# Spare rows of the direct key tiles carry 48 further key columns, with new planner thresholds

## The chip, the core and the metric

The kernel runs on one core of a Trainium2 chip. The metric is the device time of one execution in microseconds (us), the median of several runs. The engines work side by side, each through its own fixed list of instructions, and wait for each other by semaphores: TensorE (PE in the profile: matmuls; PEld: its weight loads), VectorE (DVE), ScalarE (ACT), GpSimd (POOL), and SyncE (SP), which issues the DMAs.

## What is computed

One transformer block in bf16 on 2048 tokens of width 640, with 32 heads of 20 columns and an MLP of width 1536. Six vectors from a conditioning vector scale, shift and gate its two halves:

```python
mod = (_silu(c) @ w_mod).reshape(c.shape[0], 6, 1, -1)
sa, ca, ga, sb, cb, gb = (mod[:, 0], ..., mod[:, 5])
h = _layernorm(x) * (1 + ca) + sa
qkv = h @ wqkv                       # 3 x 32 heads x 20
p = softmax(q @ k^T * 20 ** -0.5)    # per head, 2048 x 2048
x = x + ga * ((p @ v) @ wo)
h = _layernorm(x) * (1 + cb) + sb
x = x + gb * (((h @ w_gate) * (h @ w_up)) @ w_down)
```

## The kernel before

**Layout.** Heads are handled in 8 sets of four. In the tile KT the four heads of a set j lie in four strips of 32 partitions, 20 of which hold the head's key columns; QT is laid out likewise, and its 12 spare rows in each strip are zero, so whatever stands in the 12 spare rows of KT is multiplied by zero. Queries come in 7 blocks (CHUNKS: 512 tokens, then six of 256), keys in 4 token blocks tc of 512. An item is one set of one query block.

**The stream of exponentials.** For each item TensorE makes scores (L1824) into two pairs of PSUM banks. ScalarE takes the exponential of two banks in one instruction (L2801) and writes bf16 into a ring PP of 16 slots. A fixed part of the scores goes to VectorE and GpSimd instead (L1851, L1887, L1895, L1892, L1907), which form the exponential from integer operations into the tiles DB and DSS. TensorE multiplies both by the values Vf (L2504) and so frees the slots. When an item is complete, VectorE transposes and normalises it (L1978, L1984, L1989, L2021) into Ocp.

**Dense work.** Everything else on TensorE is cut into rounds: several steps that accumulate in one PSUM bank, then an evacuation by VectorE (or by ScalarE, when it has nothing else). There are rounds for the transposed activations hT (L1390), for keys and queries, for values (wV), for the gates (wmb), and for each query block a suffix: output projection (wo), layer norm, gate and up projection (stg or stx), down projection (wd), store. Rounds of column-tiled matmuls (L1233, L1429, L1493) run four strips of 32 columns side by side. The last block's suffix uses whole matmuls (L1229), and its layer-normed and transposed input is the tile h2Tc.

**How keys get into KT.** Set 0 is direct: `kq_round` (L1429) multiplies hT by four strips of 32 weight columns, each beginning at a head's first column, and the evacuation (L1442, L1443) writes the result straight into KT. The 12 extra columns of a strip are the first columns of the next head, and nobody uses them. The other seven sets are packed: `packed_round` (L1493) makes 128 columns at a time, five steps a round, from column k_base on; VectorE copies them to KPA (L1502), SP writes them to a scratch in HBM (k_rows, L1539), and one read for each set and token block brings them back in the layout of KT (L1557). With k_base = 80 there are 560 columns left: four blocks of 128 and one of 48 for each token block. A read waits for all writes of its token block issued so far.

**The order of the work.** The order of every engine's list is decided when the program is built, by a planner (class Sched) that plays the kernel through event by event with assumed durations. Whenever TensorE is free, it chooses: the next score visit, a dense piece (`pick_x`) or value products (`pv_issue`). Thresholds steer this choice. XFIRST puts dense pieces first while at least so many slot pairs of PP are free; XCONT does it for a round already begun; HOLD lets TensorE wait for a score bank soon to come free; PVMIN, PVMAX, PVCAP and PVTOL size a batch of value products. STAGE gives thresholds by item, and SEGT overrides them in segments of SEG = 8 exponentials, about 100 in all. Dense rounds have a queue key, need(x) = 13 + 10x with x in items, and a gate: the number of exponentials that must have been planned first. The packed key round of block b and token block tc has x = j0 + tc/4 - K_LEAD with K_LEAD = 0.652, where j0 is the first set that needs the block; value rounds of the second part have x from 2.02 up; the gate rounds (wmb) 2.32 and 2.37. Ten query rounds (LATEQ) and all suffix rounds have higher keys, and run in what is left.

Of the kernel before, what the change touches and what calls it, by code (L numbers as in the profile page):

```python
# [7 lines left out]
ALU = mybir.AluOpType  # L8
# [483 lines left out]
def emit_program(nc, sched, nsem_dma=56):  # L492
# [286 lines left out]
    1: {"PVTOL": 152.9, "XFIRST": 5},  # L779
    2: {"EAGER": 5},  # L780
    3: {"LKTOL": 409.9, "PVMAX": 4},
    5: {"HOLD": 18.3, "X_HALF": 186.9},
    6: {"PVCAP": 10, "PVTOL": 128.9, "XCONT": 2, "XDPRIO": 1.229},
    7: {"D_LATE": 18, "D_RES": 15, "HOLD": 49.8, "PVCAP": 18},
    9: {"HOLD": 75.5, "XBACK": 2},
    10: {"EAGER": 14, "HOLD": 75.5, "TPRIO": 0.516, "XBACK": 0},
    11: {"EAGER": 11, "PVTOL": 20.3, "XCONT": 3, "XG": -8},
    12: {"EAGER": 6, "PVTOL": 25.5, "XDPRIO": 1.926},
    13: {"HOLD": 90.7, "XG": 9},
    14: {"PV_OPEN": 1, "XBACK": 2, "XCONT": 6, "XG": -2},  # L790
    16: {"EAGER": 11, "PVTOL": 31.8, "XCONT": 4},
    17: {"D_RES": 22, "PVTOL": 373.5, "STEAL_GAP": 131.6},
    18: {"D_RES": 22, "LKTOL": 422.8, "PVMAX": 8, "PVMIN": 7, "PVTOL": 373.5, "STEAL_GAP": 131.6},
    20: {"PVTOL": 309.1, "XCONT": 0, "XG": 9},
    21: {"HOLD": 53.2, "PVMIN": 3, "PVTOL": 86.9},
    22: {"D_RES": 49, "PVCAP": 6},
    24: {"HOLD": 52.6},
    25: {"D_LATE": 13, "PV_KEEP": 3},
    26: {"EAGER": 12, "STEAL_GAP": 219.1, "XCONT": 5},
    27: {"XBACK": 2, "XG": -5},  # L800
    28: {"XCONT": 4},
    29: {"D_RES": 18, "EAGER": 15, "HOLD": 1.1, "XFIRST": 2},
    31: {"PVMAX": 6, "XDPRIO": 0.985},
    33: {"XCONT": 2, "XG": 3},
    34: {"HOLD": 14.4, "PVTOL": 187.4},
    36: {"D_LATE": 18, "EAGER": 8, "TPRIO": 0.426},
    37: {"D_LATE": 18, "EAGER": 8, "TPRIO": 0.426, "XCONT": 3},
    38: {"D_LATE": 18, "EAGER": 8, "HOLD": 14.3, "LKTOL": 40.3, "TPRIO": 0.723, "XCONT": 3, "XG": 4},
    39: {"D_LATE": 18, "EAGER": 8, "LKTOL": 40.3, "PV_OPEN": 3, "TPRIO": 0.723, "XCONT": 3, "XG": 4},
    40: {"EAGER": 6, "PVMIN": 6},  # L810
    41: {"EAGER": 3, "XFIRST": 3},
    42: {"EAGER": 4, "PV_OPEN": 1},
    43: {"XG": 14, "X_LATE": 69.8},
    44: {"EAGER": 14, "XFIRST": 5},
    45: {"EAGER": 14, "XFIRST": 5},
    46: {"D_LATE": 22, "D_RES": 20, "HOLD": 148.8},
    47: {"D_LATE": 22, "HOLD": 148.8, "PVMAX": 3, "XG": -2},
    48: {"EAGER": 2},
    49: {"EAGER": 5, "PVCAP": 15, "PV_KEEP": 4, "X_LATE": -212.0},
    50: {"EAGER": 11, "LKTOL": 38.6, "PVCAP": 15, "PV_KEEP": 4, "XDPRIO": 0.893, "X_LATE": -212.0},  # L820
    51: {"PVMIN": 5, "XBACK": 3, "XDPRIO": 0.768},
    52: {"HOLD": 97.6, "PV_OPEN": 3},
    53: {"XBACK": 2},
    54: {"HOLD": 148.1},
    55: {"PVMAX": 9, "PVMIN": 7, "PVTOL": 138.0, "TPRIO": 0.846},
    56: {"HOLD": 2.5, "PVMAX": 9, "PVMIN": 7, "PVTOL": 138.0, "PV_OPEN": 3, "TPRIO": 0.846, "X_HALF": 88.4, "X_LATE": -103.8},
    57: {"HOLD": 2.5, "PVMAX": 9, "PVMIN": 7, "PVTOL": 138.0, "PV_OPEN": 3, "TPRIO": 0.846, "X_HALF": 88.4, "X_LATE": -103.8},
    58: {"HOLD": 59.0},
    59: {"PVMAX": 4, "PV_KEEP": 1},
    60: {"PVCAP": 9, "XCONT": 2},  # L830
    61: {"LKTOL": 659.0, "PV_KEEP": 2},
    62: {"HOLD": 161.6, "XDPRIO": 1.236, "X_LATE": 20.3},
    64: {"PVCAP": 11, "PVMIN": 7, "XG": 10},
    65: {"EAGER": 10, "PVMIN": 3, "TPRIO": 0.795},
    66: {"HOLD": 0, "X_HALF": 144.4},
    67: {"EAGER": 14, "PVMAX": 13, "PV_KEEP": 2},
    68: {"EAGER": 5, "PVMAX": 13, "PV_KEEP": 2, "XG": -6, "X_LATE": 52.7},
    69: {"X_LATE": 187.0},
    70: {"HOLD": 9.6, "X_HALF": 37.7},
    72: {"HOLD": 202.6, "PV_OPEN": 3, "XDPRIO": 1.458},  # L840
    74: {"PVMIN": 5, "PV_KEEP": 4, "XG": 6},
    75: {"EAGER": 6, "HOLD": 0, "PVMIN": 2},
    76: {"LKTOL": 45.1, "PVMIN": 5, "PVTOL": 121.2},
    77: {"LKTOL": 45.1, "PVMIN": 5, "PVTOL": 121.2},
    81: {"X_LATE": 207.1},
    82: {"D_LATE": 37, "EAGER": 13, "XDPRIO": 0.618, "XFIRST": 2, "X_LATE": 207.1},
    83: {"XDPRIO": 1.036, "XFIRST": 4},
    84: {"STEAL_GAP": 206.3, "XCONT": 5},
    85: {"D_LATE": 5, "LKTOL": 647.8, "PV_KEEP": 4, "STEAL_GAP": 206.3, "XCONT": 5, "XG": 11},
    86: {"PVTOL": 117.5, "XBACK": 1, "XCONT": 2, "XFIRST": 4},  # L850
    87: {"PVMIN": 3, "PVTOL": 378.0, "XBACK": 0, "XCONT": 4},
    88: {"HOLD": 193.8},
    89: {"EAGER": 4, "HOLD": 193.8, "PVCAP": 17, "XG": -4},
    91: {"PVMIN": 3, "PV_KEEP": 2, "X_HALF": 0.7},
    93: {"PVCAP": 7, "PVMAX": 9, "X_LATE": -4.5},
    94: {"HOLD": 60.0, "PVCAP": 15, "PVMAX": 9, "X_LATE": -4.5},
    95: {"HOLD": 197.8, "PVCAP": 15, "PVMAX": 5, "PV_KEEP": 1, "X_LATE": -4.5},
    96: {"HOLD": 197.8, "PVCAP": 15, "PVMAX": 5, "PV_KEEP": 1, "XCONT": 5, "X_LATE": -4.5},
    97: {"PVMAX": 10},
    98: {"X_LATE": -11.0},  # L860
    99: {"PVMAX": 3, "XCONT": 3, "X_HALF": 4.5},
}
XG = 0
WO_GATE = 60
# [16 lines left out]
def build_kernel(nc, A_x, A_wqkv, A_wo, B_x, B_w_gate, B_w_up, B_w_down, c, w_mod, out):  # L881
# [197 lines left out]
    def dve(dur, f, deps=(), prio=3.0, **k):  # L1079
        return sc.add(Task("dve", dur, f, deps, prio=prio, **k))  # L1080
# [325 lines left out]
    kt_ready = {}  # L1406
    kt_half = {}
# [15 lines left out]

    def kq_round(kind, j, tc, prio, gate=0):
        wx = wk_sb if kind == "K" else wq_sb
        w0 = 80 * j
        mms = []
        for k in range(KD):
            f = [lambda e, b, k=k, s=s: e.matmul(  # L1429
                ps[32 * s:32 * s + 32, b, :], wx[:, k, w0 + DH * s:w0 + DH * s + 32], hT[tc][:, k, :],  # L1430
                tile_position=(0, 32 * s), start=(k == 0), stop=(k == KD - 1), skip_group_check=True) for s in range(4)]
            mms.append((C512, f))
# [29 lines left out]
        r = Round(mms, hd + w_deps(kind, j) + xd, after, prio, gate=gate, name=f"{kind}{j}.{tc}", pdeps=pd, split=split)  # L1462
# [16 lines left out]
    k_writes = {}  # L1479

    def k_base(tc):
        return 80 * KDJ if tc in K_DIRECT else 0
# [4 lines left out]
    def packed_round(kind, b, tc, prio, gate=0, late_q=False):  # L1487
# [59 lines left out]
        if kind == "K":  # L1547
            for j in range(NSET):
                top = min(80 * j + 91, D - 1)
                if 80 * j >= k_base(tc) and r0 <= top < r0 + w:  # L1550
                    dps = [x for l in done for x in l] + ([r_sb.last, r_cb.last] if j >= 4 else [])
                    kt_ready[(j, tc)] = [dma("sp", 32 * 1024, lambda e, j=j, s=s: e.dma_start(
                        KT[32 * s:32 * s + 32, j, tc * 512:(tc + 1) * 512],
                        KS[656 * tc + 80 * j + DH * s:656 * tc + 80 * j + DH * s + 32, :]),
                        dps, prio=1.1 + .01 * (j + tc / 4), dur=480.0) for s in range(4)]
                    for t in kt_ready[(j, tc)]:
                        t.whole = (kt_ready[(j, tc)], lambda e, j=j, tc=tc: e.dma_start(  # L1557
                            KT[:, j, tc * 512:(tc + 1) * 512],
                            bass.AP(KS.tensor, (656 * tc + 80 * j) * 512, [[DH * 512, 4], [512, 32], [1, 512]])))
# [476 lines left out]
    def suffix(ci):  # L2036
# [36 lines left out]
        for tl in range(ntl):  # L2073
# [30 lines left out]
            bn = []  # L2104
            for hf in range(2):
                bn.append(dve(ps_cost(320), lambda e, tl=tl, hf=hf: e.bn_stats(  # L2106
                    st2[:, tl, 6 * hf:6 * hf + 6], xck[:, tl, 320 * hf:320 * hf + 320]), [ev[hf]], prio=LN2T if tail else LN2P))
            ag = dve(115, lambda e, t=t, tl=tl: e.bn_aggr(mv2[:, t, :], st2[:, tl, :]), bn, prio=LN2T if tail else LN2P)
            f1 = lambda e, t=t: e.tensor_scalar(sd2[:, t:t + 1], mv2[:, t, 1:2], EPS, None, op0=ALU.add)
# [566 lines left out]
    def d_attach(ts, t, pos, rows, limit, relax):  # L2676
        n = 0
        got = []
        while n < limit:
# [34 lines left out]
            got.append((pick, b, st_, tu))  # L2714
# [4 lines left out]
        for pick, b, st_, tu in got:  # L2719
# [353 lines left out]
```

## Time and profile before

| what | value |
|---|---|
| median of 3 runs | 795.71 us (795.64 to 795.74) |
| the profiled execution | 795.55 us |
| its span | 793.8 us |
| dense key matmuls L1493, hT by wk | 360 |
| direct key matmuls L1429, hT by wk | 80 |
| granted TensorE clock | 1.0 in every slice |

The span runs from the first to the last instruction. The profile lists busy times of each engine, the chain of work that ended last, groups of instructions by line and shape, waits, and a timeline. All of these are from one execution, whose own time is the 795.55 us above. A matmul's duration is longer than the time by which it keeps the next one back, since matmuls are pipelined; what a matmul adds is read from the distance of successive ones.

### The profile page before, as it was taken

Reading aid. Unit: us, or ns where it says so; the run is one execution under the profiler, and the core shown is the slowest. Engines: PE = TensorE matmul, PEld = TensorE weight load, DVE = VectorE, ACT = ScalarE, POOL = GpSimd, SP = SyncE. Lnnn points to the kernel's source line nnn. Section 1 sums busy time; section 2 is a strip of 40 time slices with the busy share of each in tenths; the row PEclk is TensorE's granted clock in tenths of the full one; section 3 lists DMA queues with packets and bytes.
Section 4 is the critical chain, followed back from the end, with each engine's and each line's share of the span. In section 5 each row is a group of like instructions: output and inputs, shape, how many; then the busy total and the mean of one; then the engine's idle time right before and its main releaser. Section 6 shows DMA issues by size and latency. Waiting matters only on the chain.

```text
span 793.8 us, 36358 instructions
## 1 busy us (share of the span) xinstructions
PE 783.9 (99%) x16556; PEld 378.9 (48%) x16556; DVE 711.2 (90%) x1317; ACT 752.4 (95%) x837; POOL 358.1 (45%) x372
## 2 busy tenths in 40 slices
PE   8999999999999999999999999999999999999998
PEld 4433433333244444445455555545554455545567
DVE  7889888988999999989999989988999999898974
ACT  6999899999999999999999999999999999999941
POOL 3334646142466555444453536336355445353510
PEclk9999999999999999999999999999999999999999
DMA  9633222102351622110033305131430146214600
GB/s 301 218 111 98 63 61 61 60 25 71 107 130 43 198 46 52 44 36 20 11 94 69 70 19 117 40 68 36 102 86 21 33 105 135 62 38 91 137 20 19
DMA packets 146090, 61.88 MB, mean 78 GB/s; under 512 B 113215, under 2 KB 145935, under 8 KB 145935
## 3 DMA queue, kind: packets, MB, share of 16 engines
q1 hardware_dynamic: 145007, 58.40, 28.5%
q8 instruction: 130, 2.13, 1.1%
q10 hardware_dynamic: 928, 1.15, 0.4%
q14 instruction: 25, 0.20, 0.1%
HBM read 50.53 MB, written 8.99 MB: 75 GB/s over the span
## 4 chain that ended last, share of the span: by engine, by line
ACT 63%; PE 33%; DVE 3%; DMA 0%; issue 0%; SPq 0%
ACT PP L2801 63%; PE ps_all L1824 10%; PE ps_all L1233 8%; PE ps_all L2504 7%; PE ps_all L1493 3%; PE ps_all L1229 3%; DVE DB L1851 1%; DMA x<-in_A_x_dram 0%; PE ps_all L1429 0%; ACT xn L1300 0%; PE ps_all L1390 0%; PE ps_all L2148 0%; DVE DSS L1887 0%; PE ps_all L2966 0%; DVE st L2106 0%
## 5 line engine op out<-in xcount | busy, mean ns | idle before, releaser
L2801 ACT ACTIVATE PP<-ps_all 128x1024 bf16<-128x1024 f32 x798 | 734.6, 1169 | 4.8 <-PE ps_all L2504 2.6
L1907 POOL TENSOR_TENSOR DSS<-DB,DSS 128x512 bf16<-128x512 bf16 x252 | 287.0, 1159 | 309.3 <-DVE DSS L1895 227.1
L1851 DVE TENSOR_SCALAR DB<-ps_all 128x512 int16<-128x512 f32 x452 | 301.9, 683 | 40.3 <-PE ps_all L1824 38.4
L1824 PE MATMUL ps_all<-QT,KT 32*128 32x256 bf16 (+2 forms) x3648 | 315.3, 286 | 3.0 <-ACT PP L2801 1.0
L1824 PEld LDWEIGHTS ps_all<-QT,KT 32*128 32x128 bf16 x3648 | 92.2, 92 | 203.7 <-ACT PP L2801 182.5
L2504 PE MATMUL ps_all<-PP,Vf 128*32 128x256 bf16 (+4 forms) x2844 | 157.6, 290 | 0.3 <-DVE Vf L1593 0.2
L1233 PE MATMUL ps_all<-h2T,stg 128*32 128x256 bf16 (+2 forms) x2784 | 119.6, 279 | 0.2 <-DVE DB L1851 0.2
L2504 PE MATMUL ps_all<-DSS,Vf 128*32 128x256 bf16 (+1 forms) x1608 | 93.3, 288 | 0.1
L2504 PEld LDWEIGHTS ps_all<-PP,Vf 128*32 128x32 bf16 (+1 forms) x2844 | 58.6, 95 | 65.3 <-issue 56.7
L1887 DVE TENSOR_SCALAR DSS<-DB 128x2048 int16<-128x2048 int16 x113 | 79.2, 701 | 0.7
L1895 DVE TENSOR_SCALAR DSS<-DB 128x2048 int16<-128x2048 int16 x113 | 78.3, 693 | 1.2 <-PE ps_all L2504 1.2
L1233 PEld LDWEIGHTS ps_all<-h2T,stg 128*32 128x32 bf16 x2784 | 59.1, 96 | 36.3 <-issue 30.6
L1233 PE MATMUL ps_all<-wd,hprod 128*32 128x320 bf16 (+1 forms) x1364 | 62.3, 280 | 0.2
L1892 DVE TENSOR_TENSOR DSS<-DB,DSS 128x2048 bf16<-128x2048 bf16 x50 | 61.8, 1238 | 0.1
L2504 PEld LDWEIGHTS ps_all<-DSS,Vf 128*32 128x32 bf16 (+1 forms) x1608 | 40.5, 96 | 16.7 <-issue 9.0
L1989 POOL TENSOR_TENSOR OTn<-OT,invT 128x160 bf16<-128x160 f32 (+1 forms) x44 | 26.5, 622 | 44.3 <-DVE invT L1984 44.3
L1233 PEld LDWEIGHTS ps_all<-wd,hprod 128*32 128x32 bf16 x1364 | 31.0, 96 | 15.1 <-issue 11.4
L1233 PE MATMUL ps_all<-wV,hT 128*32 128x160 bf16 x1280 | 36.1, 234 | 0.0
L1493 PE MATMUL ps_all<-hT,wk 128*32 128x512 bf16 (+1 forms) x360 | 32.4, 382 | 0.0
L1493 PE MATMUL ps_all<-hT,wq 128*32 128x512 bf16 x375 | 31.3, 383 | 0.0
L1233 PE MATMUL ps_all<-wo,Ocp 128*32 128x320 bf16 (+1 forms) x656 | 30.2, 282 | 0.3 <-DVE DB L1851 0.2
L1233 PEld LDWEIGHTS ps_all<-wV,hT 128*32 128x32 bf16 x1280 | 23.4, 96 | 13.0 <-issue 8.3
(128 smaller groups left out, 513.8 us busy)
## 6 DMA issues: line engine op xcount, KB each, us to landing
stg<-in_B_w_gate_dram SPq DMA_DIRECT2D x74, 160.0 KB, 2.5
stg<-in_B_w_up_dram SPq DMA_DIRECT2D x74, 160.0 KB, 2.8
KT<-k_rows SPq DMA_DIRECT2D x28, 128.0 KB
QT<-q_rows SPq DMA_DIRECT2D x48, 64.0 KB, 2.1
wm<-in_w_mod_dram SPq DMA_DIRECT2D x3, 800.0 KB, 6.2
x<-in_A_x_dram SPq DMA_DIRECT2D x7, 320.0 KB
k_rows<-KPA SPq DMA_DIRECT2D x16, 128.0 KB, 2.7
wd<-in_B_w_down_dram SPq DMA_DIRECT2D x1, 1920.0 KB
```

The source lines that it names most:

```text
L1229: return lambda e, b: e.matmul(ps[:, b, c0:c0 + n], lhs(), rhs(), start=st, stop=sp)
L1233: return lambda e, b: e.matmul(ps[32 * x:32 * x + 32, b, c0 + o:c0 + o + w], lhs()[:, 32 * x:32 * x + 32], rhs() if w == n else rhs()[:, o ...
L1493: f = [lambda e, b_, k=k, x=x: e.matmul(ps[x:x + min(32, w - x), b_, :], wx[:, k, r0 + x:r0 + min(x + 32, w)], hT[tc][:, k, :], tile_posit ...
L1824: ems.append(lambda e, i=i, kt=kt: e.matmul(dstf()[:, i * u.n:(i + 1) * u.n], KT[32 * u.s:32 * u.s + 32, u.j, kt * 128:(kt + 1) * 128], QT ...
L1851: return e.tensor_scalar(DBl[st_["slot"]][:, x * 512:(x + 1) * 512], bank(cell["b"]), EBIAS, 0.0, op0=ALU.add, op1=ALU.max)
L1887: return e.tensor_scalar(DSl[st_["ss"][0]][:, :], DBl[st_["slot"]][:, :], 0x7F, 0x3F00, op0=ALU.bitwise_and, op1=ALU.bitwise_or)
L1892: return e.tensor_tensor(d, DBl[st_["slot"]][:, :].bitcast(BF16), d, ALU.mult)
L1895: return e.tensor_scalar(DSl[st_["ss"][1]][:, :], DBl[st_["slot"]][:, :], 0x7F80, 2, op0=ALU.bitwise_and, op1=ALU.bitwise_or)
L1907: return e.tensor_tensor(d, DBl[st_["slot"]][:, x * w:x * w + w].bitcast(BF16), d, ALU.mult)
L1989: return lambda e: e.tensor_tensor(OTn[:, g0:g0 + gn, DH * (j + x):DH * (j + x) + DH, :].rearrange("p b c r -> p b r c"), OT[:, nq_ * x:nq ...
L2504: ems.append(lambda e, i=i, kt=kt, stt=stt, stp=stp: e.matmul(ps[32 * s:32 * s + mc, binfo["bank"], c0:c0 + u.n], Vf[:, (kt * H + 4 * u.j ...
L2801: return e.activation(o, ps[:, b0:b0 + nu, :], AFT.Exp, scale=ESCALE)
```

## The change

The direct round of set 0 gets a weight tile of its own, wkp, in which the 12 spare columns of each strip hold columns 80 to 127 (12 for each of the four strips). Two GpSimd copies build it from wk once the first half of wk has landed. The evacuation is the same; the spare rows of KT now hold those 48 key columns, and four DMAs for each token block write them to their place in the scratch. The packed blocks start at column 128, and there are four of 128 for each token block. The first set that needs a block becomes 1, 3, 4, 6 (it was 1, 2, 4, 5, 7).

```diff
+WKP_PRIO = 0.5
+P1_TWO = 0
+KPACK = (0, 1, 2, 3)
+LN2_POOL = ()
...
+    wkp_c = []
+    wkp = alloc("wkp", [128, KD, 128], BF16) if KPACK else None
+
+    def pack_wk():
+        wkp4 = wkp[:, :, :].rearrange("p k (s c) -> p k s c", c=32)
+        for o, w, c0 in ((0, DH, 0), (DH, 32 - DH, 4 * DH)):
+            wkp_c.append(pool(KD * 4 * w * .9 + 150, lambda e, o=o, w=w, c0=c0: e.tensor_copy(
+                wkp4[:, :, :, o:o + w], wk_sb[:, :, c0:c0 + 4 * w].rearrange("p k (s c) -> p k s c", c=w)),
+                [d_wk[0]], prio=WKP_PRIO))
+
     def kq_round(kind, j, tc, prio, gate=0):
         wx = wk_sb if kind == "K" else wq_sb
         w0 = 80 * j
+        pk = kind == "K" and j == 0 and tc in KPACK
+        wst = DH
+        if pk:
+            wx, w0, wst = wkp, 0, 32
+            if not wkp_c:
+                pack_wk()
...
-                ps[32 * s:32 * s + 32, b, :], wx[:, k, w0 + DH * s:w0 + DH * s + 32], hT[tc][:, k, :],
+                ps[32 * s:32 * s + 32, b, :], wx[:, k, w0 + wst * s:w0 + wst * s + 32], hT[tc][:, k, :],
...
-        r = Round(mms, hd + w_deps(kind, j) + xd, after, prio, gate=gate, name=f"{kind}{j}.{tc}", pdeps=pd, split=split)
+        r = Round(mms, hd + (wkp_c if pk else w_deps(kind, j)) + xd, after, prio, gate=gate, name=f"{kind}{j}.{tc}", pdeps=pd, split=split)
+        if pk:
+            k_writes.setdefault(("K", tc), []).append([dma("sp", 12 * 1024, lambda e, s=s: e.dma_start(
+                KS[656 * tc + 80 + 12 * s:656 * tc + 92 + 12 * s, :],
+                KT[32 * s + DH:32 * s + 32, 0, tc * 512:(tc + 1) * 512]), list(r.evac), prio=1.0, dur=480.0) for s in range(4)])
...
     def k_base(tc):
-        return 80 * KDJ if tc in K_DIRECT else 0
+        return 128 if tc in KPACK else 80 * KDJ if tc in K_DIRECT else 0
...
-                if 80 * j >= k_base(tc) and r0 <= top < r0 + w:
+                if j >= (KDJ if tc in K_DIRECT else 0) and r0 <= top < r0 + w:
```

The table SEGT is replaced as a whole: 83 entries become 100, from a search that carries sixteen plans along. Entries with XFIRST above zero go from 8 to 17, with XCONT from 17 to 29, with PVMIN from 15 to 23; HOLD from 25 to 24, and EAGER stays at 25. Two lines of each as examples:

```diff
-    9: {"HOLD": 75.5, "XBACK": 2},
-    10: {"EAGER": 14, "HOLD": 75.5, "TPRIO": 0.516, "XBACK": 0},
+    9: {"EAGER": 15, "LKTOL": 462.9, "PVTOL": 356.7, "XFIRST": 3},
+    10: {"PVMIN": 5, "XBACK": 1, "XCONT": 3, "X_HALF": 134.5},
```

The diff also adds two branches that its own constants switch off: with LN2_POOL = () the second layer norm stays on VectorE, and with P1_TWO = 0 two score evacuations aren't joined into one.

More of the change, by code (lines that the diff above doesn't have):

```diff
@@ L2103, in suffix @@
             t = t0 + tl
[L2104 to L2109, printed above, removed]
@@ L2718, in d_attach @@
             n += 1
-        for pick, b, st_, tu in got:
+        if P1_TWO and len(got) == 2 and got[0][2] is got[1][2]:
+            got.sort(key=lambda g_: g_[0].quad[1])
+            (ua, ba, st_, ta, ra), (ub, bb, _, tb, rb) = got
+            if ba > bb:
+                ba, bb = bb, ba
+                ta.deps, tb.deps = unit_score_deps(ua) + rb, unit_score_deps(ub) + ra
+            (pa, ca), (pb, cb) = ua.task, ub.task
+            ca["b"], cb["b"] = ba, bb
+            ca["two"] = ((ba, ua.quad[1]), (bb, ub.quad[1]))
+            ca["pool"], ca["ks"] = G, (ba, bb)
+            pa.dur = ps_cost(1024)
+            pa.deps = [ta, tb] + st_["brel"]
+            for x in pb.users:
+                x.deps = [d for d in x.deps if d is not pb]
+                x.nleft -= 1
+            pb.users = []
+            st_["p1"][ub.quad[1]] = pa
+            sc.left -= 2
+            sc.add(pa)
+            return [ta, tb]
+        for pick, b, st_, tu, _ in got:
             tp, cell = pick.task
```

208 lines of the change are left out of this document (122 added, 86 removed).

## The prediction

> **What bounds the kernel now.** I read the page first: the span, the busy times, then the chain that ended last.
>
> ```profile
> span 793.8 us, 36358 instructions
> PE 783.9 (99%) x16556; PEld 378.9 (48%) x16556; DVE 711.2 (90%) x1317; ACT 752.4 (95%) x837; POOL 358.1 (45%) x372
> ACT 63%; PE 33%; DVE 3%; DMA 0%; issue 0%; SPq 0%
> L2801 ACT ACTIVATE PP<-ps_all 128x1024 bf16<-128x1024 f32 x798 | 734.6, 1169 | 4.8 <-PE ps_all L2504 2.6
> ```
>
> Two engines are full and the chain alternates between them: ScalarE with the exponentials (734.6 / 798 = 0.92 us each in the stream) and TensorE. So the question for each stretch is which of the two is late. The windows view, restricted to the exponentials (columns: window, its length, busy us and count), tells it:
>
> ```profile
> 20.00:40.00 20.00, 13.74 (x16) 1.00 0.70 221
> 80.00:95.00 15.00, 12.52 (x14) 1.00 0.24 66
> 95.00:217.00 122.00, 121.95 (x135) 1.00 0.21 61
> 217.00:307.00 90.00, 89.69 (x98) 1.00 0.38 102
> 307.00:762.00 455.00, 453.38 (x494) 1.00 0.28 64
> ```
>
> From 95 to 762 us exponentials run with 0.05 + 0.31 + 1.62 = 1.98 us of holes in 667. Nothing that TensorE saves there can be seen before the last exponential. Time can come only out of the start, the one hole at 80 to 95 us (2.48 us), and the tail behind the last exponential. The timeline of the hole and of the tail (start, length, instructions):
>
> ```profile
> 75.09 0.61 PE L1493 MATMUL ps_all<-hT,wk 128*32 128x512 bf16 x8
> 87.57 0.85 PE L1233 MATMUL ps_all<-wmb,SCb 128*32 128x320 bf16 x20
> 88.67 1.94 ACT L2801 ACTIVATE PP<-ps_all 128x1024 bf16<-128x1024 f32 x2 [1.87 <-PE ps_all L2504]
> 89.07 0.94 PE L1233 MATMUL ps_all<-wV,hT 128*32 128x160 bf16 x38
> 90.41 0.33 PEld L2504 LDWEIGHTS ps_all<-PP,Vf 128*32 128x32 bf16 x6 [0.38 <-DVE Vf L1593]
> ...
> 754.32 7.69 ACT L2801 ACTIVATE PP<-ps_all 128x1024 bf16<-128x1024 f32 x8
> 766.66 1.35 DVE L2138 TENSOR_SCALAR h2Tc<-ps_all,mcol 128x128 bf16<-128x128 bf16 x5 [0.21 <-PE ps_all L2126]
> 769.10 1.68 PE L1233 MATMUL ps_all<-wd,hprodt 128*32 128x320 bf16 x44
> 770.71 2.35 PE L1229 MATMUL ps_all<-h2Tc,stx 128*128 128x128 bf16 x39
> 773.34 17.79 PE ps_all L1229 x261
> ```
>
> The hole at 86.8 to 88.7: an exponential waits 1.87 us for the value product (L2504) to give back PP slots, and the product waits for V columns whose rounds (wV) are only then being run, behind dense key rounds (to 75.7) and the gate rounds (wmb). TensorE was late with dense work.
>
> The tail: the last exponential ends at 754.32 + 7.69 = 762.01. The input of the last block's MLP, h2Tc, is complete at 766.66 + 1.35 = 768.01, but its first matmul starts at 770.71, right behind the down-projection of the block before (wd, hprodt). From 770.71 TensorE is full to 773.34 + 17.79 = 791.13 (last row: the chain, by time). So leftover dense work delays the end by 770.71 - 768.01 = **2.70 us**. Is that leftover a backlog that reaches far back? The output stores of successive blocks (SP queue, by time) say yes:
>
> ```profile
> 542.01 9.13 SPq L2370 DMA_DIRECT2D out_dram<-xck  x2
> 616.06 14.20 SPq L2370 DMA_DIRECT2D out_dram<-xckb  x2
> 686.18 19.50 SPq L2370 DMA_DIRECT2D out_dram<-xck  x2
> 765.90 5.83 SPq L2370 DMA_DIRECT2D out_dram<-xckt  x2
> ```
>
> They end at 551.1, 630.3, 705.7 and 771.7: steps of 79, 75 and 66 us, while a block of about 98 exponentials takes 90. Each block's MLP begins as the one before ends. Dense work is a queue that TensorE works off without a break, so what leaves it early arrives at its end.
>
> **The change, part by part.** *Removed:* one packed key round per token block, 48 columns wide, four in all.
>
> ```profile
> L1493 PE MATMUL ps_all<-hT,wk 128*16 128x512 bf16 x20 | 6.8, 380 | 0.0
> L1502 DVE CAST KPA<-ps_all 48x512 bf16<-48x512 f32 x4 | 2.7, 668 | 0.2 <-PE ps_all L1493 0.2
> k_rows<-KPA SPq DMA_DIRECT2D x4, 48.0 KB, 2.2
> 23.10 1.08 PE ps_all L1493 x20
> 166.59 0.38 PE L1493 MATMUL ps_all<-hT,wk 128*32 128x512 bf16 x2
> 167.37 0.60 PE L1493 MATMUL ps_all<-hT,wk 128*32 128x512 bf16 x4
> ```
>
> The 20 narrow (16-column) matmuls are the second strip of 4 rounds of 5 steps. A full round of 5 steps with four strips adds 1.08 us to the chain. A narrow round has two strips a step, and a second step of two adds 0.60 - 0.38 = 0.22 us, as 1.08 / 5 does, since the strips run beside each other. So the saving is 4 x 1.08 = **4.32 us** of TensorE, not half. VectorE loses 4 copies of 0.668 = 2.7 us, off the chain (DVE 3%): I count nothing.
>
> *Moved:* the remaining key blocks start at column 128 instead of 80, and are needed later: block 1 by head set 3 instead of 2, block 3 by set 6 instead of 5. The queue key is (need + token block / 4 - 0.652), so block 1's four rounds move from keys 1.35 to 2.10 to keys 2.35 to 3.10. They leave the stretch ahead of the late V rounds (keys 2.02 and up), worth again 4 x 1.08 = 4.32 us of TensorE before 88 us. The hole there is 1.87 us, so I let it go. What is late next there is the gate work and the score rounds at TensorE's own pace; the other holes of that window, 2.48 - 1.87 = 0.61 us, stay. The moved rounds land in 95 to 217 us, which loses four others.
>
> *Added at the start:* two GpSimd copies that pack 128 key columns into wkp, and the first key round waits for them instead of for the weights.
>
> ```profile
> SPq L1131 <- DMA wk<-in_A_wqkv_dram: 2.8, 1, 2.8
> 10.74 0.37 SPq L1131 DMA_DIRECT2D wV<-in_A_wqkv_dram  x1
> 12.61 0.77 PEld L1429 LDWEIGHTS ps_all<-hT,wk 128*32 128x32 bf16 x20 [0.50 <-ACT hT L1396]
> 12.62 0.72 POOL L1699 COPY SCb<-scol 128x640 bf16<-128x640 bf16 x1 [3.71 <-ACT hT L1396]
> L1907 POOL TENSOR_TENSOR DSS<-DB,DSS 128x512 bf16<-128x512 bf16 x252 | 287.0, 1159 | 309.3 <-DVE DSS L1895 227.1
> ```
>
> SP waits 2.8 us for the wk load, and then issues wV at 10.74, so the weights are there at about 10.7. The copies move 400 and 240 elements a partition, together as many as the SCb copy: at least 0.72 us; at the rate of the pool's multiply (1159 ns for 512) 1.45 us. In pieces of 20 and 12 elements I take 1.0, nearest the copy. They end between 11.5 and 12.2, and the key round waits for hT until 12.61 anyway: the cover is hT, 0.4 to 1.1 us of it is left, and beyond it each microsecond costs one. Queued behind the copies on GpSimd is SCb, which itself waits until 12.62. Cost: nothing.
>
> *Added DMAs:* sixteen writes of 12 rows from KT to the scratch, 4 per token block, against four 48-row writes less.
>
> ```profile
> L1539 SPq DMA_DIRECT2D k_rows<-KPA x24: 303/324/612, 24.8 to 186.6; - x24
> 15.69 0.81 SPq L1131 DMA_DIRECT2D wk<-in_A_wqkv_dram  x1
> 22.93 1.25 PE L1493 MATMUL ps_all<-hT,wk 128*32 128x512 bf16 x20
> 31.68 0.57 SPq L1557 DMA_DIRECT2D KT<-k_rows  x1
> ```
>
> An issue takes 0.324 us, so 1.3 us of SP per token block. SP waits there for the key evacuation; behind the first four stand the second halves of the weights (from 15.69), and the first packed key round needs them at 22.93. These are 7.2 us apart, of which the load itself takes a part that no row shows; I take the 1.3 as hidden, and up to 1.3 once if it isn't. The head-set reads (first at 31.68) now wait for these writes too, which land, if issued at about 15, by 15 + 1.3 + 2.2 = 18.5. Cost: nothing.
>
> *The new thresholds* move every choice (scores, value products, dense pieces) in all four queues. No row prices that; the ends are in the rivals. The branches LN2_POOL and P1_TWO are switched off and cost nothing.
>
> **The sum.** Queue of dense work: the last MLP could start at 770.71 - 4.32 = 766.39. Its input: 768.01 - 1.87 = 766.14. The later rules: 766.39, a gain of 4.32 us, with both limits within 0.25. The profiled execution took 795.55 us (span 793.8 and 1.75 around it), 0.16 below the median shown, so the forecast is 795.71 - 4.32 = **791.4 us**. If the hole stays, the input rules and the gain is 2.70: 793.0.
>
> **Rivals.** *(1) Nothing to feel.* A PE at 99% need not be the limit.
>
> ```profile
> PEld ps_all L1824 <- ACT PP L2801: 182.5, 667, 0.5
> ```
>
> The weight loads of the scores stand 182.5 us for exponentials to release a bank, 0.27 us a time; freed dense time could become more of this wait, and the new table could redraw holes of the old size. Then 795.7, within 1.6 us. The row does not say whether TensorE was idle in that wait or emptying its pipeline; the evenly spaced blocks and the delay of 2.70 us speak against it. The Trainium skill ("Trainium Kernel Development and Optimization", Performance Expectations) says the same as this rival, that matmul busy time is a bad metric and the busy share of weight loads a good one. By that rule (48% here) TensorE has room, and the time would stay at about 795.7; the tail row at 770.71 disagrees.
>
> *(2) Slower: dense rounds ahead of value products.* XFIRST, which puts dense pieces first while enough PP slots are free, is set in 17 segments of 8 exponentials instead of 8. Where a value product then comes too late, the ring runs full and an exponential waits as at 88 us, 1.87 us a time, and this goes straight to the end. Against a gain of 4.32 it needs (4.32 + 1.6) / 1.87 = 3.2, so from the fourth such hole the kernel is slower: 795.71 - 4.32 + 4 x 1.87 = 798.9. For it: the whole table is new, and the order is fixed before the chip runs it. Against: such a wait occurs at one place of this size in 800 now.
>
> *(3) More than the removed rounds.* If the new order also spends less of TensorE on changing between scores and products, the exponentials are the limit: all holes gone (2.48 + 1.98) and the 2.70 of the tail, 7.2 us: 788.5. For it: TensorE's queue is the only reason for the tail. Against: holes of 1.98 in 667 us are nearly the floor already.
>
> *(4) The packing is late*: beyond the cover of 0.4 us, or the sixteen writes hold the weights up. 1.3 us back: 792.7, which is inside the forecast's own range (791.4 less 1.5, plus 2.4).
>
> **How the numbers follow.** Forecast with (4) 0.54, (3) 0.20, (1) 0.14, (2) 0.12. Low end: rival 3 and 1.5 of the 6.26 us without exponentials in 20 to 40 us, 787.0; high end: three holes of rival 2 and no more, 791.4 + 5.6 = 797.0. About 0.2% (1.6 us) is what a measurement of this kernel can tell from no change: faster 0.74, same 0.14, slower 0.12.
>
> **What would show it.** Dense key matmuls (L1493 from hT, wk) fall from 360 to 320, the 16-column form gone; exponentials again about 798. The holes of 80 to 95 us fall from 2.48 to about 0.6. The first matmul on h2Tc starts at about 766.4 and follows the previous down-projection by little. The first key round still starts at about 12.6 with hT as releaser. Wrong: new waits of exponentials for L2504, h2Tc complete long before its matmul, or the same tail with TensorE's score waits grown by 4 us.

## The result, and the profile after

The changed kernel takes **786.54 us** (median of 4 runs, 786.49 to 786.70) against 795.73 (795.64 to 795.82) beside it: a ratio of 0.9885, with a 95% interval of 0.9868 to 0.9902. It is 9.2 us faster. The prediction said 791.4 with 787.0 to 797.0; the time lies below that range. All times here and below are medians of runs at a granted clock of 0.996 or more; one run of e4 (below), at 0.655, took 998.26 us and is not counted.

The page of the changed kernel, its head and the groups that answer to those shown of before (the exponentials are now L2875, the scores L1865, the value products L2558, the rounds L1250, L1254, L1467 and L1534):

```profile
span 784.7 us, 36327 instructions
PE 775.1 (99%) x16556; PEld 376.3 (48%) x16556; DVE 721.1 (92%) x1330; ACT 750.3 (96%) x836; POOL 286.1 (36%) x310
L2875 ACT ACTIVATE PP<-ps_all 128x1024 bf16<-128x1024 f32 x798 | 733.5, 1145 | 4.0 <-PE ps_all L2558 1.9
L1534 PE MATMUL ps_all<-hT,wk 128*32 128x512 bf16 x320 | 24.7, 383 | 0.0
```

There are 798 exponentials as before, and the 40 matmuls of the narrow key rounds are gone (360 to 320). That the count of all matmuls is the same is chance, since other dense pieces are cut differently (those of h2T with stg and the like at L1254 are 2840, before 2784 at L1233). TensorE is as full as it was, 99%. GpSimd is less busy (358.1 to 286.1 us), since the new order gives more of the multiplications of DSS to VectorE (188 on GpSimd instead of 252). Neither busy share tells a reader that 9 us are gone.

The exponentials by window do (window, its length, busy us and count, granted clock, DMA share, GB/s):

```profile
20.00:40.00 20.00, 14.86 (x17) 1.00 0.66 203
40.00:80.00 40.00, 38.72 (x43) 1.00 0.38 111
80.00:95.00 15.00, 14.85 (x17) 1.00 0.20 49
95.00:217.00 122.00, 121.61 (x133) 1.00 0.27 79
217.00:307.00 90.00, 89.98 (x99) 1.00 0.34 89
307.00:755.00 448.00, 446.60 (x488) 1.00 0.27 62
```

The hole at 80 to 95 us has shrunk from 2.48 to 0.15 us, and 20 to 40 us holds 14.86 instead of 13.74; a new hole of 1.28 stands at 40 to 80. Up to 755 us nothing else has changed by more than 0.35. The rest is in the tail, here by its timeline:

```profile
754.00 0.31 PE L1250 MATMUL ps_all<-wo,Ocp 128*128 128x320 bf16 x1
757.36 1.94 ACT L2875 ACTIVATE PP<-ps_all 128x1536 bf16<-128x1536 f32 x2 [0.40 <-PE ps_all L2558]
759.91 1.35 DVE L2192 TENSOR_SCALAR h2Tc<-ps_all,mcol 128x128 bf16<-128x128 bf16 x5 [0.44 <-PE ps_all L2180]
761.32 1.24 PE L1250 MATMUL ps_all<-h2Tc,stx 128*128 128x128 bf16 x19 [0.75 <-DVE h2Tc L2192]
```

The last exponential ends at 757.36 + 1.94 = 759.30 (before: 762.01, 2.71 later). The first matmul on h2Tc starts at 761.32 (before: 770.71), and what it waited for is h2Tc itself. So the **lag** from the last exponential to this matmul fell from 8.70 to 2.02 us. 2.71 + 6.68 = 9.39 us; the spans differ by 793.8 - 784.7 = 9.1. From this matmul on both kernels do the same: 23.1 us to the end of the span before, 23.4 now. One sum therefore holds the whole result: end of the last exponential, plus lag, plus about 23.3.

Why the lag fell: the output projection of the last block (wo, Ocp) starts at 754.00, 5.3 us ahead of the end of the exponentials. Before it started at 761.66, only 0.35 ahead of it:

```profile
761.66 2.60 PE L1229 MATMUL ps_all<-wo,Ocp 128*128 128x320 bf16 x18 [0.19 <-ACT PP L2801]
```

From there to the first matmul on h2Tc it is 7.3 us now and was 9.05, of which 2.70 were the leftover down-projection. So 4.95 of the 6.68 us come from the earlier start and 1.73 from the shorter way.

### The profile page after: what moved, and what is told of

Read it like the earlier page. It is cut to its first block, busy times and chain, and to the rows that moved or that the text cites. A ratio compares the mean times of both kernels' runs of the same rounds, so it can differ in the third digit from the quotient of the medians.

```text
span 784.7 us, 36327 instructions
## 1 busy us (share of the span) xinstructions
PE 775.1 (99%) x16556; PEld 376.3 (48%) x16556; DVE 721.1 (92%) x1330; ACT 750.3 (96%) x836; POOL 286.1 (36%) x310
## 4 chain that ended last, share of the span: by engine, by line
ACT 65%; PE 33%; DVE 1%; DMA 1%; issue 0%; SPq 0%
ACT PP L2875 64%; PE ps_all L1865 11%; PE ps_all L1254 10%; PE ps_all L2558 6%; PE ps_all L1250 3%; PE ps_all L1534 1%; PE ps_all L1467 1%; PE ps_all L1411 1%; DMA x<-in_A_x_dram 1%; PE ps_all L1275 0%; PE ps_all L3040 0%; ACT xn L1321 0%; PE ps_all L3068 0%; DVE h2Tc L2192 0%; PE ps_all L2202 0%
## 5 line engine op out<-in xcount | busy, mean ns | idle before, releaser
L2875 ACT ACTIVATE PP<-ps_all 128x1024 bf16<-128x1024 f32 x798 | 733.5, 1145 | 4.0 <-PE ps_all L2558 1.9
L1948 POOL TENSOR_TENSOR DSS<-DB,DSS 128x512 bf16<-128x512 bf16 x188 | 214.0, 1156 | 317.7 <-DVE DSS L1936 278.4
L1892 DVE TENSOR_SCALAR DB<-ps_all 128x512 int16<-128x512 f32 x452 | 301.2, 683 | 24.8 <-PE ps_all L1865 23.1
L1865 PE MATMUL ps_all<-QT,KT 32*128 32x256 bf16 (+2 forms) x3648 | 315.3, 286 | 3.3 <-ACT PP L2875 2.1
L1865 PEld LDWEIGHTS ps_all<-QT,KT 32*128 32x128 bf16 x3648 | 92.3, 92 | 198.1 <-ACT PP L2875 174.5
L2558 PE MATMUL ps_all<-PP,Vf 128*32 128x256 bf16 (+3 forms) x2844 | 155.1, 290 | 0.0
L1254 PE MATMUL ps_all<-h2T,stg 128*32 128x256 bf16 (+2 forms) x2840 | 122.3, 276 | 0.0
L2558 PE MATMUL ps_all<-DSS,Vf 128*32 128x256 bf16 (+3 forms) x1608 | 90.2, 287 | 0.0
L2558 PEld LDWEIGHTS ps_all<-PP,Vf 128*32 128x32 bf16 (+1 forms) x2844 | 56.4, 95 | 61.6 <-issue 57.4
L1933 DVE TENSOR_TENSOR DSS<-DB,DSS 128x2048 bf16<-128x2048 bf16 x66 | 80.5, 1222 | 0.3
L1254 PEld LDWEIGHTS ps_all<-h2T,stg 128*32 128x32 bf16 x2840 | 61.6, 96 | 32.0 <-issue 27.0
L1254 PE MATMUL ps_all<-wd,hprod 128*32 128x320 bf16 (+1 forms) x1352 | 61.0, 282 | 0.0
L2558 PEld LDWEIGHTS ps_all<-DSS,Vf 128*32 128x32 bf16 (+1 forms) x1608 | 41.2, 96 | 14.4 <-issue 7.9
L1254 PEld LDWEIGHTS ps_all<-wd,hprod 128*32 128x32 bf16 x1352 | 29.3, 96 | 17.5 <-issue 13.5
L1254 PE MATMUL ps_all<-wV,hT 128*32 128x160 bf16 x1280 | 36.0, 234 | 0.8 <-DVE DB L1892 0.5
L1254 PEld LDWEIGHTS ps_all<-wV,hT 128*32 128x32 bf16 x1280 | 23.1, 96 | 15.7 <-issue 9.5
L1534 PE MATMUL ps_all<-hT,wq 128*32 128x512 bf16 x375 | 30.1, 384 | 0.0
L1254 PE MATMUL ps_all<-wo,Ocp 128*32 128x320 bf16 (+1 forms) x648 | 29.9, 283 | 0.0
L1844 POOL TENSOR_TENSOR wd<-wd,gab 128x640 bf16<-128x640 bf16 x12 | 16.8, 1398 | 21.9 <-DVE DSS L1936 13.7
```

Source lines behind the costliest of these rows:

```text
L1254: return lambda e, b: e.matmul(ps[32 * x:32 * x + 32, b, c0 + o:c0 + o + w], lhs()[:, 32 * x:32 * x + 32], rhs() if w == n else rhs()[:, o ...
L1534: f = [lambda e, b_, k=k, x=x: e.matmul(ps[x:x + min(32, w - x), b_, :], wx[:, k, r0 + x:r0 + min(x + 32, w)], hT[tc][:, k, :], tile_posit ...
L1865: ems.append(lambda e, i=i, kt=kt: e.matmul(dstf()[:, i * u.n:(i + 1) * u.n], KT[32 * u.s:32 * u.s + 32, u.j, kt * 128:(kt + 1) * 128], QT ...
L1892: return e.tensor_scalar(DBl[st_["slot"]][:, x * 512:(x + 1) * 512], bank(cell["b"]), EBIAS, 0.0, op0=ALU.add, op1=ALU.max)
L1933: return e.tensor_tensor(d, DBl[st_["slot"]][:, :].bitcast(BF16), d, ALU.mult)
L1948: return e.tensor_tensor(d, DBl[st_["slot"]][:, x * w:x * w + w].bitcast(BF16), d, ALU.mult)
```

## The experiments

Two questions. Is it the packing or the new table of thresholds that pays? And is time on TensorE worth anything by itself, as the prediction's sum assumed?

**One without the other (e1 to e4).** Three kernels with another table and one without the packing:

e1 is the changed kernel with the table of before, e4 the changed kernel and e3 the kernel before without any table:

```diff
-SEGT = {
-...
-}
+SEGT = {}
```

(in e1 the table of before stands in place of the empty one). e2 is the changed kernel with its table and without the packing:

```diff
-KPACK = (0, 1, 2, 3)
+KPACK = ()
```

> The packed spare rows with the old threshold table. Theory A (the removed rounds carry the gain: 4.3 us less TensorE work moves a queue that gets only about 0.3 us of dense work per us, so far more than 4.3 us of queue time): 788 to 792 us, the hole at 80 to 95 us smaller. Theory B (the new table carries the gain, and a table fits only the plan it was searched on): 794 to 798 us.

> The new threshold table without the packing (KPACK empty), so with the four 48-column rounds back. Theory A: 791 to 796 us, as the rounds come back. Theory B: if the table's choices are good in themselves, 787 to 790 us; if it fits only its own plan, 794 us or more.

> The kernel before without any segment table (thresholds by item only). Both theories: slower than 795.7, some 800 to 812 us; it is the base for the next run.

> The packed spare rows without any segment table. Against the run without table and without packing, theory A: 3 to 9 us faster; theory B: within 2 us.

| kernel | structure | table | us | ratio to before (95%) |
|---|---|---|---|---|
| before | old | its own | 795.64 | 1 |
| e1 | packed | of before | 824.87 | 1.0380 (1.0355 to 1.0405) |
| e2 | old | of after | 843.06 | 1.0594 (1.0578 to 1.0610) |
| e3 | old | none | 828.56 | 1.0413 (1.0398 to 1.0429) |
| e4 | packed | none | 824.95 | 1.0366 (1.0346 to 1.0387) |

A table is worth 33 to 38 us (e3 against before, e4 against after), and only with the structure that it was searched for: on the other one it is worth nothing (e1 against e4) or does harm (e2 against e3). Most expectations missed: e1 lies 27 us above both theories, e3 17 us above its range, and of the rest only "fits only its own plan" (e2) and theory A's 3 to 9 us (e4) came out.

The waits of the exponentials for value products (us, times, longest) show where the time goes, here in e2:

```profile
ACT PP L2875 <- PE ps_all L2558: 47.9, 10, 8.9
```

Before had 2.6 us in three times, the longest 1.9. Now single waits last up to 8.9 us: without fitting thresholds the ring of PP slots runs full, which is rival 2 at a size that the prediction did not think of. In e1, e3 and e4 these waits are 20.1, 25.6 and 18.8 us, the larger part of what those lose and not all of it. So swapping parts can't divide the 9.2 us. The one like pair here, no table on either side, gives the packing 828.56 - 824.95 = 3.6 us.

**Time on TensorE alone, in a fixed order (e5, e6, e9, e10).** The planner runs unchanged, and only then are instructions taken out of its list or doubled in it, so no choice moves. In e5 and e9 four of five accumulation steps of a key round are left out.

```diff
     end = sc.run()
+    nar = {}
+    for t_ in sc.order["pe"]:
+        if t_.name.startswith("Kp4."):
+            nar.setdefault(t_.name, []).append(t_)
+    for l_ in nar.values():
+        for t_ in l_[:-1]:
+            t_.emits = []
```

This is e5: Kp4 are the four narrow rounds, and the step that is kept starts the sum. e9 does it to the rounds Kp3 of the changed kernel, the last of each token block. e6 and e10 take the rounds Kp3 too, and have in place of the last two lines:

```diff
+        l_[0].emits = l_[0].emits * 6
```

> The kernel before, same table and same order of every queue; of the four narrow key rounds only the last of five steps is issued, so the last 48 key columns hold one fifth of their sum. 4 x 4 x 0.22 = 3.5 us of TensorE leave, in place. Theory A (the prediction's: dense work is a queue that TensorE works off without a break, so what leaves it arrives at its end): 795.6 - 3.5 = 792.1. Theory B (the removed time pays only where the planner can move other work into it): what is freed becomes waiting for exponentials, 795.0 to 795.8, and the wait of the score weight loads for exponentials (182.5 us in the kernel before) grows by about 3.

> The changed kernel, same table and order; the first step of the last key round of each token block is issued six times instead of once (it overwrites, so the output is unchanged): 4 x 5 x 0.22 = 4.4 us of TensorE come back, about what the packing removed. Theory A: 786.5 + 4.4 = 790.9. Theory B: the waits for exponentials swallow it, 786.3 to 787.5; more only if one of the four places has no slack.

> The changed kernel, same table and order; of the last key round of each token block only the last of five steps is issued, so the last 128 key columns hold one fifth of their sum: 4 x 4 x 0.22 = 3.5 us of TensorE leave in place. It stands against e6, where 4.4 us added at the same four places cost 3.9. If the order is tight there (what is added is paid, what is taken away is gained): 786.5 - 3.5 x 3.9 / 4.4 = 783.4. If it sits just at its limit (paid one way only, as e5 says of the kernel before): 786.1 to 786.7.

> The kernel before, same table and order; the first step of the last full key round of each token block is issued six times instead of once (output unchanged): 4.4 us of TensorE added in place. If its order sits at its limit as that of the changed kernel (e6): 795.6 + 3.9 = 799.5. If it has room there, which would explain why e5 gained nothing: 795.6 to 796.6.

| kernel | edit in place | us (ratio to before, 95%) | against its base |
|---|---|---|---|
| e5 | before, less 3.5 us | 795.67 (1.0004, 0.9995 to 1.0013) | 0.0 |
| e9 | after, less 3.5 us | 786.47 (0.9885, 0.9870 to 0.9900) | -0.1 |
| e6 | after, plus 4.4 us | 790.43 (0.9933, 0.9919 to 0.9948) | +3.9 |
| e10 | before, plus 4.4 us | 799.39 (1.0047, 1.0032 to 1.0062) | +3.8 |

The 3.5 and 4.4 us are estimates, 0.22 us a step as the prediction read it. What is taken out of an order in place brings nothing; what is put in costs nearly all of itself. In e5 TensorE's busy time did fall, by 3.6 us, and nothing else moved. Its page, and its exponentials by window (95 to 217 us, where before had 121.95):

```profile
PE 780.3 (98%) x16524; PEld 378.4 (48%) x16524; DVE 711.2 (90%) x1317; ACT 752.4 (95%) x837; POOL 358.2 (45%) x372
```

```profile
95.00:217.00 122.00, 121.95 (x134) 1.00 0.20 61
```

In e6 and e10 the same window has 118.15 and 118.80, that is 3.5 and 3.2 us of new holes, and they reach the end. The rows of e6, of its windows and its waits (us, times, longest; after had 1.8 us in 5 times):

```profile
95.00:217.00 122.00, 118.15 (x129) 1.00 0.25 75
```

```profile
ACT PP L2875 <- PE ps_all L1865: 5.3, 9, 1.0
```

and those of e10 (before had 1.7 us in 6 times for this wait):

```profile
95.00:217.00 122.00, 118.80 (x130) 1.00 0.20 59
```

```profile
ACT PP L2801 <- PE ps_all L1824: 4.7, 10, 0.8
```

e9 and e10 came out as the limit would have it, on either kernel. In this window exponentials had hardly a hole (0.05 us before, 0.39 after), so there was nothing to win, and the order of what follows is fixed, so the freed time could not be used later. That added time is paid says that there was hardly any slack either: both orders stand at their limit at these places. Theory B said the first for e5 and missed e6, since it expected a slack there. One detail of it fell too: the wait of the score weight loads did not grow (182.5 in e5 as before); the freed time shows nowhere but in TensorE's lower busy time.

**The same search for both structures (e7, e8, e11 to e14).** Since a table fits one structure only, the structures are compared each with a table searched in the same way: a beam over the segments of eight exponentials that begins without thresholds, carries 14 plans (32 in e13 and e14), tries 12 (16) sets of thresholds on each, drawn from the values that occur in the two tables, and ranks them two segments later by the planner's time and the work done. The pairs differ in seed, and the third in width.

e7, e11 and e13 are the kernel before, e8, e12 and e14 the changed kernel, each with only the lines of SEGT replaced:

```diff
 SEGT = {
-...
+...
 }
```

> The kernel before without any packing, with thresholds searched anew from none (for this kernel and for e8 by the same beam search of equal width, trials and seed, which carries 14 plans). Theory S (the structure makes the gain, the search only re-fits the table): its old table was the result of a search too, so it stays at 795.6 within 1.6. Theory T (a better search makes most of it; the structure is worth what it was with neutral thresholds, 828.56 - 825.18 = 3.4): 786.5 + 3.4 = 789.9, within 2.

> The changed kernel with thresholds searched anew exactly as for e7. Theory S: 9 us below e7. Theory T: 2 to 4.5 us below e7, so between 786 and 790. If it is not below e7 at all, the removed rounds are worth nothing that a table can't give.

> As e7, the beam search begun from another seed. Theory T: as e7, 791.0 within 1.5. A table's luck alone: anywhere between 786 and 796.

> As e8, with e11's seed. If the structure is worth 2.6 to 3.4 (e7 less e8; e3 less e4), this is 2 to 4 below e11. If that difference was the tables' luck, it can be anything from -2 to +5, and the worth of the structure has to be given with that spread.

> As e7, a third seed, and the beam carries 32 plans instead of 14. Theory T: a wider search of the old structure still ends near e7 and e11, 791 within 1.5. If the search's width is what counts: 788 to 789.

> As e8, with e13's seed and width. e13 less this is the third value of the structure's worth (2.58 and 0.36 so far, 3.38 with neutral thresholds): 1 to 4 if these are one quantity with a spread; 4.32 would fit the prediction's sum. Exponentials done by 95 us: 1.9 us more than in e13, as in the three pairs with a fitted table (1.89, 1.91, 1.85).

| pair | old structure | packed | difference |
|---|---|---|---|
| e7, e8 | 791.00 (0.9941, 0.9926 to 0.9956) | 788.42 (0.9909, 0.9892 to 0.9925) | 2.6 |
| e11, e12 | 791.16 (0.9944, 0.9929 to 0.9959) | 790.80 (0.9944, 0.9927 to 0.9960) | 0.4 |
| e13, e14 | 792.30 (0.9957, 0.9943 to 0.9972) | 787.86 (0.9904, 0.9887 to 0.9920) | 4.4 |
| before, after | 795.73 | 786.54 | 9.2 |

The old structure gains 3.4 to 4.6 us from another table (each against before beside it). The packing, searched alike, is worth 0.4 to 4.4 us, 2.5 on average; the pair without tables (3.6) lies among these. The 0.4 is no more than the spread of e12's own runs (790.74 to 791.89), and e13's runs spread by 1.6 us. No table found here reaches that of the changed kernel: 786.5 against 787.9 to 790.8. So the 9.2 us are, by averages of three pairs that differ much, 795.7 - 791.5 = 4.2 for a better search of the old structure, 791.5 - 789.0 = 2.5 for the packing, and 789.0 - 786.5 = 2.5 for a better table of the packed one. Which table a search happens on is worth as much as the packing. What the old structure would reach with a search like the one behind the changed kernel's table stays open.

Theory S falls: it had e7 at 795.6 and e8 9 us below it. Theory T holds for the three old kernels, and the wider beam of e13 did not help. Its value for the packing holds on average only: e12 missed its 2 to 4, and e14 gave more than expected, 4.4 where 1 to 4 was one theory and the 4.32 of the prediction's sum the other, with 3.5 us more exponentials by 95 us instead of 1.9. With three values from 0.4 to 4.4, neither is confirmed.

Where each of them acts is read from the sum (the end of the last exponential, plus lag, plus about 23.3) and from how far the exponentials are at 95 us. First the windows view for the exponentials of the first 95 us (the third number is their busy time), of before and of after:

```profile
0.00:95.00 95.00, 69.52 (x75) 1.00 0.54 163
```

```profile
0.00:95.00 95.00, 71.41 (x78) 1.00 0.52 159
```

The same window of e7, e8, e11, e12, e13 and e14, each followed by three rows of that kernel's timeline: the run of exponentials that ends last, the first output projection of the last block (wo, Ocp), and the first matmul on h2Tc. e7:

```profile
0.00:95.00 95.00, 69.92 (x76) 1.00 0.54 164
```

```profile
758.28 2.03 ACT L2796 ACTIVATE PP<-ps_all 128x512 bf16<-128x512 f32 x2 [0.87 <-PE ps_all L1819]
759.21 2.62 PE L1224 MATMUL ps_all<-wo,Ocp 128*128 128x320 bf16 x18
765.96 0.34 PE L1224 MATMUL ps_all<-h2Tc,stx 128*128 128x128 bf16 x3 [0.46 <-DVE h2Tc L2133]
```

e8:

```profile
0.00:95.00 95.00, 71.83 (x78) 1.00 0.53 160
```

```profile
755.77 2.17 ACT L2854 ACTIVATE PP<-ps_all 128x512 bf16<-128x512 f32 x2 [0.50 <-PE ps_all L1844]
756.54 2.62 PE L1229 MATMUL ps_all<-wo,Ocp 128*128 128x320 bf16 x18
763.04 1.35 PE L1229 MATMUL ps_all<-h2Tc,stx 128*128 128x128 bf16 x21
```

e11:

```profile
0.00:95.00 95.00, 68.83 (x74) 1.00 0.53 162
```

```profile
754.63 7.50 ACT L2802 ACTIVATE PP<-ps_all 128x1024 bf16<-128x1024 f32 x8 [1.36 <-PE ps_all L2505]
758.11 0.45 PE L1230 MATMUL ps_all<-wo,Ocp 128*128 128x320 bf16 x2
...
766.11 0.34 PE L1230 MATMUL ps_all<-h2Tc,stx 128*128 128x128 bf16 x3 [0.46 <-DVE h2Tc L2139]
```

e12:

```profile
0.00:95.00 95.00, 70.68 (x77) 1.00 0.53 159
```

```profile
738.76 21.57 ACT L2852 ACTIVATE PP<-ps_all 128x1024 bf16<-128x1024 f32 x23
759.03 2.62 PE L1227 MATMUL ps_all<-wo,Ocp 128*128 128x320 bf16 x18
765.53 1.12 PE L1227 MATMUL ps_all<-h2Tc,stx 128*128 128x128 bf16 x17 [0.88 <-DVE h2Tc L2169]
```

e13:

```profile
0.00:95.00 95.00, 68.37 (x75) 1.00 0.54 162
```

```profile
751.96 9.27 ACT L2804 ACTIVATE PP<-ps_all 128x1024 bf16<-128x1024 f32 x10 [0.39 <-PE ps_all L1827]
760.78 2.62 PE L1232 MATMUL ps_all<-wo,Ocp 128*128 128x320 bf16 x18
767.28 0.23 PE L1232 MATMUL ps_all<-h2Tc,stx 128*128 128x128 bf16 x1
```

e14:

```profile
0.00:95.00 95.00, 71.82 (x78) 1.00 0.53 160
```

```profile
754.30 2.86 ACT L2866 ACTIVATE PP<-ps_all 128x1024 bf16<-128x1024 f32 x3 [0.40 <-PE ps_all L1856]
755.81 2.62 PE L1241 MATMUL ps_all<-wo,Ocp 128*128 128x320 bf16 x18
762.30 1.35 PE L1241 MATMUL ps_all<-h2Tc,stx 128*128 128x128 bf16 x21
```

| kernel | exponentials by 95 us | last one ends | first wo ahead of that end | lag to h2Tc's first matmul | that matmul | span |
|---|---|---|---|---|---|---|
| before | 69.52 | 762.01 | 0.35 | 8.70 | 770.71 | 793.8 |
| after | 71.41 | 759.30 | 5.30 | 2.02 | 761.32 | 784.7 |
| e7 old | 69.92 | 760.31 | 1.10 | 5.65 | 765.96 | 789.3 |
| e8 packed | 71.83 | 757.94 | 1.40 | 5.10 | 763.04 | 786.5 |
| e11 old | 68.83 | 762.13 | 4.02 | 3.98 | 766.11 | 789.4 |
| e12 packed | 70.68 | 760.33 | 1.30 | 5.20 | 765.53 | 789.0 |
| e13 old | 68.37 | 761.23 | 0.45 | 6.05 | 767.28 | 790.9 |
| e14 packed | 71.82 | 757.16 | 1.35 | 5.14 | 762.30 | 785.9 |

Three things are to be seen. *First*, from the first matmul on h2Tc it is 23.1 to 23.6 us to the end of the span in all eight: what lies behind it hardly differs. *Second*, with a fitted table the packed structure has always done more exponentials by 95 us, 1.9 us more in three pairs and 3.5 in the fourth, and in the three searched pairs the stream then ends 2.4, 1.8 and 4.1 us earlier (2.7 after against before). There the packing shows, as far as four pairs can tell. It doesn't come by itself: without a table it wasn't so, e4 had done 65.91 us by then and e3 67.76, and the 3.6 us between those two came another way. *Third*, the lag goes by the table, not by the structure: 2.0 to 8.7 us, and in all eight it is the shorter, the earlier the first output projection starts. The pair e11, e12 shows it best: the packed kernel's stream ends 1.8 us earlier, its lag is 1.2 longer, and 0.4 us of difference is left. The table of the changed kernel has the shortest lag of all; that is 6.7 of its 9.4 us. The timelines show the link: in the six kernels where 18 of the projection's matmuls run in one piece, the first five pieces of h2Tc are complete 6.3 to 6.7 us after it starts (before 768.01 - 761.66 = 6.35, e8 762.84 - 756.54 = 6.30), and the first matmul on h2Tc follows within 0.2 us, in before alone 2.70 later. In after and e11, which spread the projection, it takes 7.3 and 8.0 us. So the lag is about this way less the head start. What in a table brings the projection forward was not taken apart.

## Why the prediction was wrong, point by point

**The bound: right.** Two engines are full, and time came only out of the first 95 us and the tail; 95 to 755 us changed by no more than 0.35 in any window.

**The hole: the size came out, in part by luck.** 1.87 us were to go; the first 95 us gained 71.41 - 69.52 = 1.89. But that is a sum of other parts: 2.33 came at 80 to 95 us and 1.12 at 20 to 40, where the prediction expected nothing; 1.28 were lost at 40 to 80, where there had been no hole, and 0.27 ahead of 20. Nor did four key rounds leave the stretch up to 88 us: 120 packed key matmuls have started by then instead of 160, which is two rounds, 2.16 us and not 4.32 (and of the four rounds that the prediction moved, one, with key 2.10, stood behind the first V key, 2.02, as it was). The new order also has the gate rounds out of the way, which before ran from 83.7 us ahead of the late V rounds; here their last row in the changed kernel:

```profile
79.58 0.32 PE L1254 MATMUL ps_all<-wmb,SCb 128*32 128x320 bf16 x4
```

How much of the hole the moved key rounds closed, and how much the earlier gate rounds, is not shown.

**The start: right.** The changed kernel's timeline:

```profile
10.80 0.84 POOL L1452 COPY wkp<-wk 128x400 bf16<-128x400 bf16 x2 [1.61 <-DMA wk<-in_A_wqkv_dram]
12.88 0.77 PEld L1467 LDWEIGHTS ps_all<-hT,wkp 128*32 128x32 bf16 x20 [0.50 <-ACT hT L1417]
14.91 1.54 SPq L1502 DMA_DIRECT2D k_rows<-KT  x4
23.21 1.26 PE L1534 MATMUL ps_all<-hT,wk 128*32 128x512 bf16 x20
```

Both copies together take 0.84 us (the estimate was 1.0) and end at 11.64, and the first key round starts at 12.88 with hT as releaser, 0.27 later than before. The copies are not the reason: an instruction ahead of them, L1327 on GpSimd, is late already by as much (7.99 us; before, L1306 at 7.71). The four writes take SP 1.54 us (1.3), and the first packed round starts 0.28 later (23.21 against 22.93). So rival 4 did not come.

**The removed rounds: the rule was wrong as it stands.** The dense key matmuls fell from 360 to 320 as counted. But "what leaves it early arrives at its end" does not hold of itself: e5 takes 3.5 us out and gains 0.0. With the order fixed, a gap in it stays a gap; time on TensorE can pay only where the planner puts something else into it. With a new plan 4.32 us were forecast, and the packing brings 0.4, 2.6 and 4.4 with tables searched alike, and 3.6 without any.

**The thresholds: the step that failed.** "The new thresholds move every choice [...]. No row prices that; the ends are in the rivals." The sum so put it at nothing, and it is the larger term. By the averages above, 6.7 of the 9.2 us are the table's (4.2 that the old structure gets too, and 2.5 more). One fitted table against another moves the old structure by 3.4 to 4.6 us and the packed one by 1.3 to 4.3. That the kernel before had a fitted table said nothing of how far it was from the best.

**The sum: the rule held, both its terms were mis-sized.** "The later rules" is what happened: the first matmul on h2Tc now follows h2Tc. But the leftover work was to end at 766.39, and the last matmuls on it now run before 754.1:

```profile
753.67 0.39 PE L1254 MATMUL ps_all<-wd,hprodt 128*32 128x160 bf16 x8
```

And h2Tc was to come 1.87 us earlier, as the stream does. It came 6.75 earlier, 768.01 against 759.91 + 1.35 = 761.26. The prediction took the way from the last exponential to h2Tc, 6.00 us before, as fixed. It is a part of the order too: 1.96 now.

**The rivals.** The time went the way of (3), "more than the removed rounds", which had 0.20, and beyond its 788.5, but not by its mechanism: the holes of 95 to 755 us, which were to go, are 1.81 us instead of 1.98. The 788.5 was taken for a floor: all holes and the 2.70 of leftover work, 7.2 us. The holes did not all go, and the tail gave 6.7 instead of 2.70; the floor left out that h2Tc itself can move. (2) did not come: exponentials wait 1.9 us in three times for value products, against 2.6 in three. (1) was wrong of this change and right of time taken from TensorE in place: in e5 and e9 its busy time falls by 3.6 and 3.3 us and the time stays. That the matmul busy share is a bad metric for how close a kernel is to roofline, as the Trainium skill says ("Trainium Kernel Development and Optimization", Performance Expectations), goes with e5 and e9. But the busy share of weight loads, which the Trainium skill calls a good metric there, stands at 48% in after too, and in e6 the 3.9 us are paid all the same. Neither share says what a change brings to an order that is cut to fit.

## What to carry to other kernels

Where a planner fixes the order and its thresholds are searched, a change that brings a new table is two changes: price the search by itself (take the old structure and search it again), and give the range of the forecast that room, here 1 to 5 us. In these two kernels time removed in place from an engine that is 99% busy was worth nothing, and otherwise what a new order could make of it; time added in place was paid nearly in full. So the two signs have to be forecast by different rules. Where a tail starts by the later of two inputs, ask of both whether the order can move them.

## What the hardware showed

VectorE's integer steps on DSS can take longer when they begin during a GpSimd multiplication. The tail of before, by its timeline:

```profile
751.47 0.68 DVE L1895 TENSOR_SCALAR DSS<-DB 128x2048 int16<-128x2048 int16 x1
752.23 1.15 POOL L1907 TENSOR_TENSOR DSS<-DB,DSS 128x512 bf16<-128x512 bf16 x1 [2.76 <-DVE DSS L1895]
752.80 1.13 DVE L1887 TENSOR_SCALAR DSS<-DB 128x2048 int16<-128x2048 int16 x1
...
756.28 2.27 POOL L1907 TENSOR_TENSOR DSS<-DB,DSS 128x512 bf16<-128x512 bf16 x2 [2.90 <-DVE DSS L1892]
757.44 1.66 DVE L1895 TENSOR_SCALAR DSS<-DB 128x2048 int16<-128x2048 int16 x1 [0.19 <-PE ps_all L2504]
```

Alone the step takes 0.68 us; begun while GpSimd multiplies it takes 1.13 and 1.66, and both times it ends 0.55 us after GpSimd (753.93 - 753.38 and 759.10 - 758.55). The whole trace of before holds 24 steps of L1887 and L1895 that begin during a multiplication, and each ends 0.55 to 0.69 us after it. The 186 steps of L1851 that do so read from PSUM, and none takes more than 0.69 us. The Trainium skill ("SBUF — State Buffer", SBUF: two separate sides) has an exclusive lock on the port pair that the two engines share, by which the later one waits for the whole instruction of the other; these rows agree. The time beyond 0.68 us adds up to 3.0 us in before and 1.3 in after; whether any of it reaches the end was not tested.
